# A recurrence followed by a three-matrix MLP on one core: the last 64 rows of the first product as pairs of matmuls in two row halves, and the second product in the inverse's banks

## The chip, the core and the metric

One NeuronCore of a Trainium2 chip runs the whole program. Its engines work side by side and meet at semaphores: TensorE (PE) multiplies, VectorE (DVE), ScalarE (ACT) and GpSimd (POOL) do elementwise work, SyncE (SP) issues most transfers. The metric is the device time of one execution in microseconds.

## The reference

```
for t in range(S):                       # S = 768, batch 4, 8 heads, head size 40
    y[:, :, t] = einsum('bhd,bhde->bhe', rt, state)
    Sa = einsum('bhde,bhe->bhd', state, at)
    state = state * wt[:, :, None, :] - einsum('bhd,bhe->bhde', Sa, bt) \
            + einsum('bhd,bhe->bhde', vt, kt)
x = y.transpose(0, 2, 1, 3).reshape(3072, 320)
out = ((x @ w1) * (x @ w2)) @ w3 @ w_out           # 320 -> 1024 -> 1024 -> 320
```

The recurrence's inputs are single precision; the MLP weights arrive as 64-bit numbers.

## The kernel before, in words

Time is cut into 12 chunks of 64 steps. For each chunk the recurrence is put as matrix products: `load` and `scale` bring in the inputs and form running products of the decay, `causal` forms the products of a and b (L551), `solve` inverts the small triangular matrices with a chain of VectorE instructions (L604 to L690), `join` extends these inverses to 64 steps with 32x32 matmuls (L753), `pairs` and `tokens` (L792, L816) prepare operands, and `rec` (L840) carries the state over, two of the four batches at a time. `gather` moves the result y by DMA into xr.

`mlp` then takes the chunk's 256 tokens. The 320 input columns lie as two tiles of 128 rows and one of 64 rows, which is laid out twice, in rows 0 to 63 and 64 to 127. Each factor is split in a high part (rounded for fast matmuls) and a low part. **The first product** (L957) sums, for each of 16 blocks of 128 outputs, eight matmuls of 128 rows and 256 columns over `terms`; the last two, (4, 2) and (4, 5), belong to the 64 rows: `WT[4]` holds their high part in rows 0 to 63 and their low part in rows 64 to 127, tile 2 of xs is x's high part and tile 5 its low part. **The second product** (L983) multiplies the elementwise product by W3, the product of w3 and w_out that is formed once (L470): 48 matmuls in two groups of 24, each group in one bank of PSUM, copied out as `o`.

Before the first product of the first chunk the weights must be there. `weights` converts the 64-bit numbers in pieces of 128 rows and 1024 columns (`convert`: two ScalarE and five elementwise instructions, L394 to L415, the last on DVE or POOL), 17 pieces in all, and splits w1 and w2 into high and low parts (L457). Six pieces are those of w1 and w2.

PSUM has 8 banks: six in the pool `bank`, which nearly all products share, and two that are the tile `ab` of the inverse.

The order of the work on each engine is not that of the code. Every operation is recorded with a due time and a cost, and `Order.place` sets the order of all engines once, in a list, from the tables `OFF`, `P`, `ON`, `OPS` and from the pools' sizes. On the chip each engine then runs its own list in order and waits at semaphores.

Of the kernel before, what the change touches and what calls it, by code (L numbers as in the profile page):

```python
# [14 lines left out]
ALU = mybir.AluOpType  # L15
# [4 lines left out]
NCH = S // C  # L20
# [12 lines left out]
SLOTS = dict(fm=4, xx=3, aa=3, lm=4, gi=1, gt=1, ab=1, TDX=1, rv=4, vg=5, un=4, bk=5, hs=2, st=2, y=1, xr=1, JP=2, TT=2, bank=6,  # L33
# [4 lines left out]
T0, T = 449.562, 122.639  # L38
P = dict(w0=116.83, ws=51.334, ld=75.808, sc=8.354, ca=161.389, so=-139.305, sp=243.519, jo=671.741, pa=42.027,
         tk=3.502, rg=-37.491, ga=1051.868, ml=179.371, mt=282.608)  # L40

ON = dict(aa="dppddpdddppdpppddppppddd", cv="pdddppdddpddddppp",
          gl="dpppdpppddppddpppdddddpppppdpdpdppppddddpppdpppp", ws="pdddpp", xs="ddpddppppdpppdddppddpdpd")
OFF = {"ca.j": -611.218, "ca.js": -295.116, "ca.lm": -409.432, "ca.mask": 322.878, "ca.mm": -196.496, "cv.e":
       -352.619, "cv.exp": -294.308, "cv.f": 875.871, "cv.in": 923.729, "cv.lo": 148.411, "cv.m": -331.453, "cv.out":
       -690.808, "cv.sign": -986.054, "ga": 652.698, "jo.cp1": 176.7, "jo.cp2": 1171.31, "jo.mm1": 500.308, "jo.mm2":
       559.977, "jo.tt": 1216.266, "ld.aa": 255.685, "ld.fm": -308.122, "ld.xx": -220.769, "m.a": -43.748, "m.ab":
       -25.534, "m.gh": -539.967, "m.gl": -14.3, "m.mm1": 97.143, "m.mm2": 289.0, "m.o": 98.802, "m.out": -533.298,
       "m.xh": -105.084, "m.xl": 349.579, "nil": 390.528, "pa.cp": -142.457, "pa.mask": 411.539, "pa.mm": 399.693,
       "pa.rv": 721.462, "pa.v": -32.743, "r.hs": -489.727, "r.n": 318.043, "r.s": -178.475, "r.sb": -189.193, "r.st":  # L50
       490.608, "r.t0": -269.903, "r.t1": 72.728, "r.t2": -860.309, "r.tr": -475.318, "r.u": -459.283, "r.y":
       -480.807, "r.zn": -15.068, "r.zv": -155.411, "sc.aa": 621.487, "sc.chk": -167.343, "sc.exp": 187.27, "sc.gi":
       -148.615, "sc.gt": -230.551, "sc.ln": 87.006, "sc.scan": 203.673, "sc.xs": 130.059, "so.d": -775.834, "so.in":
       -264.37, "so.m1": -358.78, "so.m2": -299.304, "so.q": 713.223, "so.sa": -515.229, "so.sb": -535.393, "so.t":
       -345.96, "so.td": 366.095, "so.tt": -385.449, "so.v": -186.183, "so.x": -90.021, "so.z": 257.847, "tk.cp":
       -717.729, "tk.mm": 348.057, "w.hi": 667.696, "w.lo": -164.398, "w3.hi": 386.505, "w3.lo": -443.484, "w3.mm":
       -484.2, "z.bk": 434.685}
LOOK = dict(pe=0.135, act=0.0, dve=0.0, pool=0.101, sp=0.0, nil=0.0)
# [1117 lines left out]
```

## Time and profile before

| | |
|---|---|
| median of 3 runs | 648.69 us (648.24 to 648.99) |
| profiled execution | 643.84 us, its span 642.1 us |
| TensorE busy | 566.2 us, 88% of the span |
| VectorE busy | 473.3 us, 74% |
| ScalarE busy | 382.5 us, 60% |
| GpSimd busy | 184.7 us, 29% |
| TensorE's granted clock, mean | 0.984 of full speed |

The span runs from the first to the last instruction; the profiled execution's own time has 1.74 us around it. Busy shares are means over stages that differ: the first quarter of the span holds the conversion of the weights, the rest the chunks' steady turn.

### The profile page before, as it was taken

To read this page: it belongs to the slowest core of one execution; us is meant where nothing else is said; L and a number is where in the kernel's file an instruction comes from. 1 tells how busy PE (TensorE), PEld (TensorE's weight loads), DVE (VectorE), ACT (ScalarE), POOL (GpSimd) and SP (SyncE) were. 2 spreads that over 40 slices of the span, in tenths; PEclk is the share of its full clock that TensorE was granted. 3 is DMA by queue.
4 is the path that set the end of the run, shared out by engine and by line. 5 is a ranking of instruction groups with operands and counts; after the bars stand their busy time and mean duration, and the time that the engine had idled before them with its cause. 6 is when DMAs were issued, how large, how long until landed. Compare 5 with 4: busy or idle time off the path is not lost.

```text
span 642.1 us, 27039 instructions
## 1 busy us (share of the span) xinstructions
PE 566.2 (88%) x11970; PEld 503.9 (78%) x11970; DVE 473.3 (74%) x849; ACT 382.5 (60%) x825; POOL 184.7 (29%) x230
## 2 busy tenths in 40 slices
PE   1536889867999999999999999998999999999995
PEld 0435767556988988888888889887988898898995
DVE  6799897987949959769589599497595794971220
ACT  6767557686465665755755746657557557354221
POOL 3542414035332413403312115332232242020111
PEclk9999989968999999999999999999999999999998
DMA  8975566535213423523534335235135333210001
GB/s 193 294 225 167 154 212 217 196 87 152 69 29 85 117 69 98 141 48 90 137 80 110 82 79 134 59 96 141 41 93 141 78 83 81 51 37 14 26 21 25
DMA packets 53401, 68.23 MB, mean 106 GB/s; under 512 B 29984, under 2 KB 37664, under 8 KB 51232
## 3 DMA queue, kind: packets, MB, share of 16 engines
q1 hardware_dynamic: 53280, 66.46, 38.3%
q8 instruction: 95, 1.56, 1.0%
q14 instruction: 26, 0.21, 0.1%
HBM read 57.79 MB, written 3.93 MB: 96 GB/s over the span
## 4 chain that ended last, share of the span: by engine, by line
PE 36%; DVE 28%; ACT 17%; DMA 9%; SPq 5%; issue 4%; POOL 0%; ACTq 0%; DVEq 0%
PE bank L957 15%; PE bank L840 9%; ACT JP L273 5%; DVE tmp L630 4%; SPq L915 4%; DMA fm<-in_fmg_dram 4%; PE bank L983 4%; ACT TT L273 3%; PE bank L551 3%; DMA xr<-y 3%; DVE ab L604 2%; PE bank L470 2%; DVE mf L408 2%; DVE ga L971 2%; ACT hs L273 2%
## 5 line engine op out<-in xcount | busy, mean ns | idle before, releaser
L957 PE MATMUL bank<-xs,W 128*128 128x256 f32 x1536 | 208.3, 288 | 2.8 <-ACT o L273 2.8
L957 PEld LDWEIGHTS bank<-xs,W 128*128 128x128 f32 x1536 | 187.8, 189 | 14.1 <-ACT o L273 3.6
L273 ACT ACTIVATE gh<-ga 128x512 fp32r<-128x512 f32 x48 | 30.3, 631 | 94.8 <-DVE ga L971 94.8
L891 DVE TENSOR_TENSOR un<-bank,mask_h 128x416 f32<-128x416 f32 x48 | 28.2, 588 | 73.0 <-PE bank L840 63.9
L974 POOL TENSOR_TENSOR gl<-ga,gh 128x512 fp32r<-128x512 f32 x29 | 37.5, 1292 | 118.3 <-ACT gh L273 92.4
L801 POOL TENSOR_SCALAR_AFFINE_SELECT vg<-vg 64x256 f32<-64x256 f32 x96 | 43.9, 457 | 74.6 <-DVE gl L974 24.0
L983 PE MATMUL bank<-W3h,gh 128*128 128x320 f32 x192 | 63.8, 332 | 0.0
L567 POOL TENSOR_SCALAR_AFFINE_SELECT lm<-lm 64x512 f32<-64x512 f32 x48 | 34.0, 708 | 95.5 <-ACT lm L273 74.7
L983 PE MATMUL bank<-W3l,gh 128*128 128x320 f32 x192 | 59.2, 308 | 0.0
L983 PE MATMUL bank<-W3h,gl 128*128 128x320 f32 x192 | 59.2, 308 | 0.0
L273 ACT ACTIVATE JP<-bank 64x256 f32<-64x256 f32 (+2 forms) x120 | 45.4, 379 | 20.7 <-PE bank L551 19.0
L840 PE MATMUL bank<-hs,TT 64*64 64x104 f32 x768 | 49.8, 269 | 7.3 <-ACT TT L273 5.2
L840 PE MATMUL bank<-un,bk 64*64 64x104 f32 (+1 forms) x768 | 47.9, 266 | 2.8 <-DVE un L891 2.3
L523 POOL TENSOR_TENSOR xx<-xx,gi 112x1024 f32<-112x1024 f32 x12 | 28.5, 2379 | 74.6 <-DVE gi L519 22.9
L971 DVE TENSOR_TENSOR ga<-bank,ga 128x512 f32<-128x512 f32 x48 | 32.7, 681 | 22.3 <-PE bank L957 22.3
L840 PEld LDWEIGHTS bank<-hs,TT 64*64 64x64 f32 x768 | 39.3, 142 | 11.5 <-ACT TT L273 6.0
L840 PE MATMUL bank<-vg,bk 64*64 64x104 f32 (+1 forms) x768 | 47.1, 264 | 0.0
L840 PEld LDWEIGHTS bank<-un,bk 64*64 64x64 f32 (+1 forms) x768 | 37.8, 130 | 8.9 <-DVE un L891 5.6
L551 PE MATMUL bank<-aa,xx 40*64 40x64 f32 x1536 | 32.8, 239 | 10.7 <-POOL xx L523 5.5
L551 PEld LDWEIGHTS bank<-aa,xx 40*64 40x64 f32 x1536 | 30.5, 153 | 12.9 <-POOL xx L523 5.7
L470 PE MATMUL bank<-wof,w3f 128*128 128x320 f32 x128 | 38.0, 453 | 2.4 <-DVE w3f L415 1.5
L273 ACT ACTIVATE ga<-bank 128x512 f32<-128x512 f32 x48 | 28.7, 597 | 16.9 <-PE bank L957 16.3
(120 smaller groups left out, 1245.9 us busy)
## 6 DMA issues: line engine op xcount, KB each, us to landing
rv<-in_rv_dram SPq DMA_DIRECT2D x48, 294.0 KB
xx<-in_fmx_dram SPq DMA_DIRECT2D x24, 448.0 KB
raw<-in_w3t_dram SPq DMA_DIRECT2D x8, 1024.0 KB
raw<-in_w_dram SPq DMA_DIRECT2D x6, 1024.0 KB
fm<-in_fmg_dram SPq DMA_DIRECT2D x24, 227.5 KB
aa<-in_fma_dram SPq DMA_DIRECT2D x24, 224.0 KB
vg<-in_vt_dram SPq DMA_DIRECT2D x48, 80.0 KB
out_dram<-o SPq DMA_DIRECT2D x48, 80.0 KB
```

The lines of the kernel that those rows point to most:

```text
L273: act.activation(out_, in_, AF.Copy, scale=scale)
L470: pe.matmul(out=pt.t[:, 0:DM], lhsT=w[:, j], rhs=wof[:, j], start=(j == 0), stop=(j == NJ - 1))
L523: e.tensor_tensor(out=X, in0=X, in1=gi.t.unsqueeze(2).to_broadcast([ROWS, 2 * NP, 2, C]), op=ALU.mult)
L551: pe.matmul(out=bank(s)[64 * z:64 * z + 64, i, p], lhsT=X[r, p, z], rhs=aa[i].t[r, p], start=True, stop=True)
L567: op("ca.mask", due + 6, lambda q=q: pool.affine_select(out=lm.t[q], in_=lm.t[q], pattern=[[0, 2 * NP], [1, C]], compare_op=ALU.is_gt, fil ...
L801: op("pa.mask", due + 2, lambda q=q, vg=vg: pool.affine_select(out=vg.t[q, :, 0:C], in_=vg.t[q, :, 0:C], pattern=[[0, NP], [1, C]], compar ...
L840: pe.matmul(out=out_(ab ^ z, p), lhsT=left(ab, ab ^ x, p), rhs=right(ab ^ x, p), start=start and p == 0, stop=True, skip_group_check=True)
L891: dve.tensor_tensor(out=un[i].t, in0=view(hp[i]), in1=mask_h.unsqueeze(1).to_broadcast([128, NP, N]), op=ALU.mult)
L957: pe.matmul(out=pt.t[:, TOK * x:TOK * x + TOK], lhsT=WT[k][:, cs], rhs=xs.t[:, z], start=(n == 0), stop=(n == 7))
L971: op("m.ab", t, lambda a=a, pt=pt: dve.tensor_tensor(out=a.t, in0=wide(pt), in1=a.t, op=ALU.mult), r=[pt], w=[a])
L974: both(("gl", c % NCH * 4 + j // 2), "m.gl", t + 1, lambda e, a=a, j=j: e.tensor_tensor(out=gl.t[:, j:j + 2], in0=a.t, in1=gh.t[:, j:j + 2 ...
L983: pe.matmul(out=pt.t[:, 0:DM], lhsT=l.t[:, j, ts], rhs=W3[r][:, j], start=(j == 0 and n == 0), stop=(j == NJ - 1 and n == 2))
```

## The change

The eighth term goes: the low part of x for the 64 rows now meets the high part of the weights alone. That product has only 64 rows, so it runs as matmuls of 64 rows: the block of w1 in row half 0 to 63 and that of w2 in row half 64 to 127, two banks at a time (`m.mm0`, four matmuls for two blocks of each, then seven terms of 128 rows for each block on top). For this `WT[4]` holds w1's high part in rows 0 to 63 and its low part below, and w2 the other way round. These 64 rows of w1 and w2 come as one piece `wc` of 128 rows instead of two pieces, so there are 16 pieces.

The second product takes its banks from a new pool `xb`, the two halves of `ab`. The solve of chunks 2 and later holds both halves, that of chunks 0 and 1 one. In the last chunk half of the output transfers are issued by ScalarE. The tables of the order are all new.

```diff
-SLOTS = dict(fm=4, xx=3, aa=3, lm=4, gi=1, gt=1, ab=1, TDX=1, rv=4, vg=5, ...
+SLOTS = dict(fm=4, xx=3, aa=3, lm=4, gi=1, gt=1, xb=2, TDX=1, rv=4, vg=5, ...
...
-T0, T = 449.562, 122.639
+T0, T = 588.06, 126.787
...
-    "m.xh": ("act", 0.9), "m.xl": ("dve", 0.95, 1), "m.mm1": ("pe", 0.95, 0, "128", 1.12, 16, 0.348, 1.88), ...
+    "m.xh": ("act", 0.9), "m.xl": ("dve", 0.95, 1), "m.mm0": ("pe", 0.25, 0, "64r", 0.43, 8, 0.08, 1.88), "m.mm1": ("pe", 0.832, 0, "128", 1.0, 14, 0.305, 1.88), ...
...
     tiles["ab"] = [ps.tile([128, 1024], F32, name="ab")]
+    tiles["xb"] = [tiles["ab"][0][:, 512 * i:512 * i + 512] for i in range(2)]
...
-            for f in range(2 * DFF // CW):
+            for f in range(2 * DFF // CW if k < 2 else 1):
                 cs = slice(CW * f, CW * f + CW)
-                mf = convert(w12[k * 128:k * 128 + 128, cs], None, due)
+                mf = convert(w12[k * 128:k * 128 + 128, cs] if k < 2 else wc, None, due)
...
+                    op("w.hi", due, f1, r=[mf, *over], w=[("W", k, x)])
+                    if k < 2:
+                        both(("ws", 2 * k + f), "w.lo", due, f2, r=[mf, *over], w=[("W", k, x)])
+                    else:
+                        op("w.lo/d", due, lambda f2=f2: f2(dve), r=[mf, *over], w=[("W", k, x)])
...
-        jp, ab, tdx = jp_[c], slot("ab"), slot("TDX")
+        jp, tdx = jp_[c], slot("TDX")
+        xbs = [slot("xb") for _ in range(1 if c < MERGED else 2)]
+        ab = xbs[0] if c < MERGED else Whole(tiles["ab"][0])
...
-    terms = [(0, 0), (0, 3), (2, 0), (1, 1), (1, 4), (3, 1), (4, 2), (4, 5)]
+    terms = [(0, 0), (0, 3), (2, 0), (1, 1), (1, 4), (3, 1), (4, 2)]
...
+            pts = [slot("bank") for _ in range(2)]
+
+            def f0(j=j, pts=pts):
+                for x in range(2):
+                    for w in range(2):
+                        q, col = slice(64 * w, 64 * w + 64), w * DFF + (j + x) * 128
+                        pe.matmul(out=pts[w].t[:, TOK * x:TOK * x + TOK], lhsT=WT[4][q, col:col + 128], rhs=xs.t[q, 5],
+                                  start=x == 0, stop=True, skip_group_check=True)
+
+            op("m.mm0", t, f0, r=[(xs, "l"), "W12"], w=pts, hold=[a, gh, gl])
...
-            pt, o = slot("bank"), slot("o")
+            pt, o = slot("xb"), slot("o")
```

What this does to the order is shown at three places. The first is TensorE's list in the steady turn. Before, a turn of the first product stands behind `join` (L753) like this, two blocks of one bank:

```order
L753 MATMUL bank_156<-TDX_119,JP_145 32x32 x32
L957 MATMUL bank_154<-xs_1832,W_0_100 128x256 x2
L957 MATMUL bank_154<-xs_1832,W_2_101 128x256
L957 MATMUL bank_154<-xs_1832,W_1_1466 128x256 x2
L957 MATMUL bank_154<-xs_1832,W_3_1467 128x256
L957 MATMUL bank_154<-xs_1832,W_4_1468 128x256 x2
L957 MATMUL bank_154<-xs_1832,W_0_100 128x256 x2
```

After, L973 is the new matmul of 64 rows, L983 what was L957, L856 what was L840:

```order
L983 MATMUL bank_155<-xs_1624,W_1_1433 128x256 x2
L983 MATMUL bank_155<-xs_1624,W_3_1434 128x256
L983 MATMUL bank_155<-xs_1624,W_4_1435 128x256
L973 MATMUL bank_153<-xs_1624,W_4_1435 128x256
L973 MATMUL bank_156<-xs_1624,W_4_1435 128x256
L973 MATMUL bank_153<-xs_1624,W_4_1435 128x256
L973 MATMUL bank_156<-xs_1624,W_4_1435 128x256
L856 MATMUL bank_158<-un_132,bk_137 64x104
L856 MATMUL bank_158<-un_132,bk_137 40x104
```

Each block has one matmul less on `W_4`, and a group of four on alternating banks stands ahead of its two banks, apart from them. Counted over the whole list up to the end of the program's normal path, the first product's matmuls of 128 rows go from 1536 to 1344, 192 of 64 rows come, and from the first of them on the stretches of one array shape (128 rows, 64 rows by 128 columns, 64 by 64, 32 by 32) number 310 where they were 262.

The second place is VectorE's list where the weights become ready. Before, the last piece's L412 is followed by the inverse of chunk 2 and by the recurrence, while POOL converts and splits the last piece:

```order
L604 STREAM_TRANSPOSE ab<-JP_144 128x1024
L412 TENSOR_TENSOR sg_165<-sg_165,e_164 128x1024
L630 TENSOR_TENSOR tmp<-GP,ab 128x4
...
L896 TENSOR_TENSOR st_140<-bank_155,fm_105 104x160
L896 TENSOR_TENSOR st_141<-bank_156,fm_105 104x160
L657 TENSOR_TENSOR tmp<-GP 128x128
L943 TENSOR_TENSOR xs_1832<-xr_143,xs_1832 128x768
```

After, L421 is that L412, L424 the last step of the conversion, L468 the split of the weights, L959 the low part of the first chunk's x:

```order
L468 TENSOR_TENSOR W_3_1434<-mf_166,W_1_1433 128x1024
L417 SCALAR_TENSOR_TENSOR mf_167<-raw_163,mf_167 128x1024
L421 TENSOR_TENSOR sg_165<-sg_165,e_164 128x1024
L424 TENSOR_TENSOR mf_167<-mf_167,sg_165 128x1024
L907 TENSOR_TENSOR un_129<-bank_158,mask_h 128x416
L468 TENSOR_TENSOR W_4_1435<-mf_167,W_4_1435 64x1024 x2
L907 TENSOR_TENSOR un_130<-bank_155,mask_h 128x416
L959 TENSOR_TENSOR xs_1624<-xr_143,xs_1624 128x768
L916 TENSOR_TENSOR y_142<-bank_157,fm_106 104x4x64
L916 TENSOR_TENSOR y_142<-bank_153,fm_106 104x4x64
L620 STREAM_TRANSPOSE ab<-JP_144 128x1024
```

The last split moved from POOL to VectorE, and chunk 2's inverse (L604, now L620) and a share of the recurrence moved behind it. Ahead of the last piece's L412 VectorE now has one piece less (four instructions, one each of L394, L404, L408, L412), two of L415, two of L891, two of L900, two of L896, one of L523 and the L604 less, and one of L457 more. TensorE's list ahead of the first product is shorter by 160 rows of L840 and 16 of L792 (each row two matmuls in the trace) and by four of L816.

The third place is VectorE's list at the turn from one inverse to the next. After, L650 is the last sum of the inverse, L706 and L709 turn it, L620 begins the next inverse in `ab`:

```order
L646 TENSOR_TENSOR tmp<-ab,GP 128x512
L650 TENSOR_REDUCE Tp<-tmp 128x8x8
L706 STREAM_TRANSPOSE TDX_119<-Tp 128x32x16
L709 STREAM_TRANSPOSE TDX_119<-TDX_119 128x512
L526 TENSOR_TENSOR aa_110<-aa_110,fm_105 112x512
L997 TENSOR_TENSOR ga_1626<-bank_153,ga_1626 128x512
L959 TENSOR_TENSOR xs_1624<-xr_143,xs_1624 128x768
L1000 TENSOR_TENSOR gl_1623<-ga_1626,gh_1622 128x512
L620 STREAM_TRANSPOSE ab<-JP_145 128x1024
L907 TENSOR_TENSOR un_129<-bank_158,mask_h 128x416
```

The rows alone stand much as they did before, but between the first and the ninth of them TensorE's 48 matmuls of the second product and ScalarE's two copies of `o` must now come and go in the same banks; before, the second product had banks of the shared pool.

## Rows read from the trace of the kernel before

**Rows 1.** The page: TensorE's busy tenths in 40 equal slices.

```profile
PE   1536889867999999999999999998999999999995
```

**Rows 2.** Windows of all engines: length, then busy us (instructions) of each, TensorE's clock, DMA.

```profile
0.00:160.00 160.00, 104.04 (x2393) 82.42 (x2394) 136.14 (x211) 109.46 (x202) 58.20 (x73) 0.95 0.66 190
160.00:590.00 430.00, 416.68 (x9128) 377.53 (x9128) 328.33 (x623) 259.91 (x601) 117.41 (x151) 1.00 0.33 85
```

**Rows 3.** The timeline where the weights become ready: start, duration, engine, line, operation.

```profile
144.90 0.68 DVE L412 TENSOR_TENSOR sg<-sg,e 128x1024 bf16<-128x1024 bf16 x1
145.73 2.13 POOL L415 TENSOR_TENSOR mf<-mf,sg 128x1024 f32<-128x1024 f32 x1 [0.74 <-DVE tmp L630]
150.49 2.35 POOL L457 TENSOR_TENSOR W<-mf,W 64x1024 fp32r<-64x1024 f32 x1 [0.18 <-ACT W L273]
156.13 0.95 DVE L943 TENSOR_TENSOR xs<-xr,xs 128x768 fp32r<-128x768 f32 x1
157.86 1.21 PE L957 MATMUL bank<-xs,W 128*128 128x256 f32 x8
```

**Rows 4.** Groups by line and shape: busy us, mean ns of one, idle before.

```profile
L394 DVE TENSOR_SCALAR e<-raw 128x1024 uint16<-128x1024 uint16 x16 | 11.2, 699 | 1.1 <-DMA raw<-in_w_dram 1.0
L408 DVE SCALAR_TENSOR_TENSOR mf<-raw,mf 128x1024 f32<-128x1024 uint32 x16 | 21.2, 1326 | 0.2
L412 DVE TENSOR_TENSOR sg<-sg,e 128x1024 bf16<-128x1024 bf16 x16 | 12.2, 760 | 3.0 <-ACT sg L401 2.4 <-ACT e L398 0.6
L415 DVE TENSOR_TENSOR w3f<-mf,sg 128x1024 f32<-128x1024 f32 x6 | 7.3, 1222 | 0.2
L891 DVE TENSOR_TENSOR un<-bank,mask_h 128x416 f32<-128x416 f32 x48 | 28.2, 588 | 73.0 <-PE bank L840 63.9 <-ACT lm L273 9.2
L900 DVE TENSOR_TENSOR y<-bank,fm 104x256 f32<-104x256 f32 x48 | 17.8, 410 | 6.1 <-PE bank L840 5.9
L896 DVE TENSOR_TENSOR st<-bank,fm 104x160 f32<-104x160 f32 x44 | 13.1, 311 | 0.0
L523 DVE TENSOR_TENSOR xx<-xx,gi 112x1024 f32<-112x1024 f32 x12 | 14.4, 1202 | 0.1
L604 DVE STREAM_TRANSPOSE ab<-JP 128x1024 f32<-128x1024 f32 x10 | 20.2, 2022 | 13.1 <-ACT JP L273 13.1
L273 ACT ACTIVATE W<-mf 128x1024 fp32r<-128x1024 f32 x6 | 6.3, 1050 | 0.6 <-DVE mf L415 0.6
```

**Rows 5.** The chain that ended last, in order of time: start, duration, what.

```profile
290.09 1.14 PE bank L957 x8
...
417.75 1.59 PE bank L840 x64
...
613.07 15.24 PE bank L957 x128
628.32 7.06 PE bank L983 x48
```

**Rows 6.** TensorE's timeline in two stretches of `rec`, which alternate between the row halves.

```profile
143.83 0.94 PE L840 MATMUL bank<-vg,lm 64*64 64x104 f32 x32 [0.17 <-ACT bk L273]
...
383.80 0.26 PE L840 MATMUL bank<-un,bk 64*40 64x104 f32 x2
383.81 0.26 PE L840 MATMUL bank<-vg,bk 64*40 64x104 f32 x2
383.89 0.26 PE L840 MATMUL bank<-un,bk 64*40 64x104 f32 x2
```

**Rows 7.** VectorE alone in one steady turn: inverse begun to turned, then up to the next.

```profile
368.30:397.50 29.20, 28.41 (x60) 1.00 0.38 99
397.50:412.50 15.00, 6.52 (x7) 1.00 0.36 89
```

**Rows 8.** The timeline's end: the last copy and the last two output transfers.

```profile
635.40 0.44 ACT L273 ACTIVATE o<-bank 128x320 f32<-128x320 f32 x1 [2.21 <-PE bank L983]
635.86 1.11 SPq L992 DMA_DIRECT2D out_dram<-o  x2
```

More of the change, by code (lines that the diff above doesn't have):

```diff
@@ L238, in place @@
             elif e == "sp":
-                done, clock[e] = max(t + FLIGHT, landed[-1]) + o["span"], t + o["cost"]
+                done, clock[e] = max(t + FLIGHT + o["cold"], landed[-1]) + o["span"], t + o["cost"]
                 landed.append(done)
+                done += o["act"]
             else:
@@ L261, in attention_moe @@
 @with_exitstack
-def attention_moe(ctx: ExitStack, tc: tile.TileContext, fmg, fmx, fma, rv, vt, sq, svr, w12, w3t, wo, out):
+def attention_moe(ctx: ExitStack, tc: tile.TileContext, fmg, fmx, fma, rv, vt, sq, svr, w12, wc, w3t, wo, out):
     nc = tc.nc
@@ L425, in convert @@
         return mf
-    pieces = iter(range(17))
+    pieces = iter(range(16))
     def weights():
@@ L445, in weights, with f1, f2 @@
                 op("nil", due, second, w=["reg2"])
-            for f in range(2 * DFF // CW):
+            for f in range(2 * DFF // CW if k < 2 else 1):
                 cs = slice(CW * f, CW * f + CW)
-                mf = convert(w12[k * 128:k * 128 + 128, cs], None, due)
-                n = (0, 1, 4)[k]
-                rows = slice(64, 128) if k == 2 else slice(0, 128)
+                mf = convert(w12[k * 128:k * 128 + 128, cs] if k < 2 else wc, None, due)
                 over = ["conv"] if k == 0 else ["conv", "reg2"]
-                def f1(mf=mf, n=n, cs=cs):
-                    copy(WT[n][:, cs], mf.t)
-                def f2(e, mf=mf, n=n, rows=rows, k=k, cs=cs):
-                    e.tensor_tensor(out=WT[2 + k][rows, cs], in0=mf.t[rows], in1=WT[n][rows, cs], op=ALU.subtract)
-                op("w.hi", due, f1, r=[mf, *over], w=[("W", k, f)])
-                both(("ws", 2 * k + f), "w.lo", due, f2, r=[mf, *over], w=[("W", k, f)])
+                for x in (f,) if k < 2 else range(2):
+                    xs = slice(CW * x, CW * x + CW)
+                    q, z = (slice(0, 128),) * 2 if k < 2 else (slice(64 * x, 64 * x + 64), slice(64 - 64 * x, 128 - 64 * x))
+                    hi, lo = (0, 1, 4)[k], 2 + k
+                    def f1(mf=mf, hi=hi, q=q, xs=xs):
+                        copy(WT[hi][q, xs], mf.t[q])
+                    def f2(e, mf=mf, hi=hi, lo=lo, q=q, z=z, xs=xs):
+                        e.tensor_tensor(out=WT[lo][z, xs], in0=mf.t[q], in1=WT[hi][q, xs], op=ALU.subtract)
+                    op("w.hi", due, f1, r=[mf, *over], w=[("W", k, x)])
[3 more added lines that the diff above has]
+                        op("w.lo/d", due, lambda f2=f2: f2(dve), r=[mf, *over], w=[("W", k, x)])
                 due += step
@@ L707, in solve @@
         for cost, fn, two in steps:
-            op("so.x", t, fn, r=[ab], w=["solve"], cost=cost, two=two)
+            op("so.x", t, fn, r=xbs, w=["solve"], cost=cost, two=two)
             t += cost * span / total
@@ L957, in f3 @@
                         pe.matmul(out=pt.t[:, TOK * x:TOK * x + TOK], lhsT=WT[k][:, cs], rhs=xs.t[:, z],
-                                  start=(n == 0), stop=(n == 7))
+                                  start=False, stop=(n == 6), skip_group_check=True)
                 for x in range(2):
@@ L991, in mlp @@
             for b in range(2):
-                op("m.out", t, lambda b=b, tt=tt, o=o: sp.dma_start(
+                tag, e = ("m.oa", act) if c == NCH - 1 and b else ("m.out", sp)
+                op(tag, t, lambda b=b, tt=tt, o=o, e=e: e.dma_start(
                     out=out[bass.ds((2 * tt + b) * S + row, C)], in_=o.t[64 * b:64 * b + 64]), r=[o])
@@ L1148, in _layout @@
     rows += [6 * D + e for e in range(8, D)] + [7 * D + e for e in range(8, D)]
-    rows += rows[256:]
     def bits(x):
```

85 lines of the change are left out of this document (45 added, 40 removed).

## The prediction

> **What bounds the kernel now.** I read the busy slices first, then windows of all engines, then the timeline where the picture changes, then the chain that ended last. The slices show a weak first quarter and a full rest [rows 1]. The windows give its size: TensorE is busy 104.0 of the first 160 us, then 416.7 of the next 430 at full clock [rows 2]. So after the first quarter TensorE bounds the kernel, with 13.3 us of gaps; before it something else does. VectorE is busy 136.1 of those 160 us, ScalarE 109.5, GpSimd 58.2 [rows 2]: the conversion of the weights, nearly all on VectorE, holds back the first product, which starts at 157.86 [rows 3]. Two things thus shorten the kernel: an earlier first product, as far as TensorE's work isn't merely moved behind it, and less TensorE time after it.
>
> In the chain, 128 matmuls of the first product take 15.24 us, 0.119 each, and 48 of the second 7.06, 0.147 each; eight of the first between stretches of another array shape take 1.14, where 8 x 0.119 is 0.95 [rows 5]. The 0.19 left over is what a change of shape costs. The recurrence starts four matmuls (each shown row stands for two) every 0.09 us [rows 6], so 64 cost 1.41 of the 1.59 that they take [rows 5], and 0.18 is left over there too. I take 0.18 a change.
>
> **The change part by part.** I cost it against the profiled execution, 643.84 us (span 642.1 and 1.74 around it); the median of the runs, 648.69, lies 4.85 above, and I carry the difference over to it unchanged.
>
> *Pairs in place of the eighth term.* Of each pair of blocks of w1 and w2, four matmuls of 128 rows go: 4 x 0.119 = 0.476 us, 48 times. Four of 64 rows come. The trace has none of that shape. Its nearest rows are the recurrence's: four matmuls of 104 columns every 0.09 us [rows 6]. One column at a time at 2.4 GHz, the higher of the clock's two levels, which the window grants [rows 2], four in turn would need 4 x 43 = 173 ns; so two must run together, and the products alternate between the row halves. Lower bound therefore: a pair costs what one does, 0.238 for the group, and 48 x 0.238 = 11.4 us are saved. Upper bound: the halves run in turn, 0.476, and nothing is saved. I take the lower, since [rows 6] are of the same kind (two row halves, alternating banks).
>
> Each of these matmuls also loads its own weights. Where all weights are 64 columns wide, 32 matmuls with their 32 loads take 0.94 us [rows 6], 0.76 without the change of shape: 2.7 columns loaded per ns. Two loads of 128 columns in 0.119 us are 2.2 per ns, so by the row the loads don't bind. The Trainium skill ("TensorE: Matmul & The Clock Gate", section LDWEIGHTS) says that a load's time goes with its columns, not its rows, columns / 1.2 in ns. By that rule two loads one after the other would take 213 ns, a group 0.43 us, and only 2 us would be saved. The trace disagrees with it for loads of two row halves, which it shows overlapping.
>
> *Changes of shape.* From the first product on, TensorE's list has 310 stretches for 262: 48 x 0.18 = 8.6 us are given back. Below, if passing from 64x64 to 64x128 is free for those groups that follow the recurrence, some 6 less; above, nothing in the trace asks for more than 0.19.
>
> *The start.* Ahead of the last piece's L412 VectorE has less to do: a piece without its last step (L394 and L404 at 0.70 each, L408 1.33, L412 0.76), two L415 (2.44), two L891 (1.18), two L900 (0.82), two L896 (0.62), an L523 (1.20), an L604 (2.02), less one L457, priced as the like-shaped L415 (1.22) [rows 4]: 11.8 - 1.2 = 10.6 us. VectorE is 85% busy there [rows 2], so I let its idle time stand and count 10.6. Behind L412, before: 11.2 us to L943, mostly two slow steps on GpSimd and another before them (2.13, 2.35) [rows 3]. After: L412 0.76, L415 1.22, ScalarE's first half 1.05, two L457 on VectorE 2.44 [rows 4], then what lies between the last split and L943, 3.3 before (150.49 + 2.35 to 156.13, [rows 3]) and at least one ScalarE copy, say 1; I take 2. Together 7.5, so 3.7 earlier (2.5 to 4.7). The first product starts 14.3 us earlier.
>
> *What the start leaves behind.* TensorE's list ahead of the first product is shorter by 176 rows of L840 and L792, 352 matmuls at 0.022: 7.7 us come after it instead. (L816's four are about made up for by the shorter 40-column ones.)
>
> *The inverse's banks.* The second product (7.06 us a chunk, [rows 5]) and the copies of `o` must fit between the last read of `ab` and the next L604, and everything in VectorE's list behind L604, the masks L891 of the recurrence first, waits with it. In a steady turn L604 to L690 takes 29.2 us, 28.4 of it busy, and 15.0 pass to the next L604, 6.5 busy [rows 7]. The new stay is 7.1 for the matmuls, 0.4 for the copy [rows 8], 3.2 for `join` (128 matmuls at 0.022 and two changes), 0.9 for a block of the recurrence between, 0.5 for changes: 12.1 of 15.0. VectorE's idle time there covers it, with 3 us to spare; cost 0, and what it takes if the cover is gone is a rival below. The banks it frees in the shared pool gain nothing by the trace's steady gaps, 13.3 us in all.
>
> *The end.* The last two transfers are issued by one queue in 1.11 us [rows 8]; two issuers save half, 0.5.
>
> Sum: -14.3 + 7.7 - 11.4 + 8.6 - 0.5 = -9.9. Profile 643.84 to 633.9; median 648.7 to **638.8 us**. Bounds of the single terms make it 632 (free changes, the start 1 us better) to 650 (pairs in turn).
>
> **The rivals.**
> - *The pairs don't overlap.* Then the 11.4 is gone: 650. For it: no such shape is in the trace. Against it: [rows 6]. Chance 0.08. The Trainium skill's rule on loads above, with both halves loaded in turn, would come out close to this, at 648.
> - *The start gains little.* If ScalarE (109 of 160 us busy) or the transfers of the raw pieces set the pace once VectorE has less between them, the first product comes 6 us earlier, not 14.3: -1.6, 647. For it: L412 already waits 3.0 us for ScalarE [rows 4]. Against: that is little in 16 pieces. Chance 0.15.
> - *Slower: the inverse and the second product wait for each other.* Place: L604 behind the copy of `o`. If TensorE gets through the 12.1 us late because its blocks wait in their turn for VectorE (L891 waits 63.9 us for TensorE over the run, [rows 4]), each microsecond beyond the 15.0 lengthens every turn, some ten of them. From 1 us a turn it eats the whole gain; at 2 us it is -9.9 + 20 = +10, 659. For it: VectorE is 97% busy in L604 to L690, so it can't catch up. Against: 3 us of room. Chance 0.16.
> - *The forecast*, 0.61, with its own range of 630 to 645.
>
> **How the numbers follow.** 638.8 is the likeliest case's time. The range 628 to 654 takes in the free changes and a better start below, the pairs in turn, the small start and half of the slower rival above. A change of 0.2% (1.3 us) is about what a measurement of this kernel can tell. Faster: the forecast (0.61), the small start (0.12 of its 0.15), part of the rest 0.03: 0.76. Same: 0.03 and 0.04 of the pairs, 0.07. Slower: 0.16 and a small rest, 0.17.
>
> **What would show it.** In the profile after: the first product starting near 143.5 instead of 157.9; groups of L973 of four matmuls that take about 0.42 with their change of shape, not 0.66; about 0.18 more for each block of the first product that they precede; a steady turn near 44 us or a little less; VectorE's wait at L620 behind ScalarE's `o` of some microseconds that costs TensorE nothing; the masks L907 not waited for longer than before. The prediction is wrong if the first product starts after 152, if L973's group takes over 0.6, or if the turn is above 45 with TensorE idle ahead of L856 while VectorE stands at L620.

## The result, and the profile after

| | before | after |
|---|---|---|
| median of the runs | 648.47 us (647.37 to 648.99) | 639.44 us (638.80 to 640.05) |
| ratio, 95% interval | | 0.9863 (0.9846 to 0.9880) |
| span of the profiled execution | 642.1 us | 638.0 us |

The change gains 9.0 us, 1.4%; 9.9 were forecast. The profiled execution of before lay 4.6 us under the median of its runs, that of after did not; so the kernel of before was run and profiled again (`before_again`, 648.2 us, span 645.7), and stretches are compared with this second profile where nothing else is said. How far one profile can mislead shows in the two of before: they differ by 1.6 us up to chunk 3's inverse and by 1.9 over the eight turns behind it.

The page of the kernel after, with the slices that answer to [rows 1] and two groups that answer to [rows 4]:

```profile
span 638.0 us, 27026 instructions
...
PE   1535988869999999999999999999999999999996
...
L907 DVE TENSOR_TENSOR un<-bank,mask_h 128x416 f32<-128x416 f32 x48 | 28.1, 585 | 30.6 <-PE bank L856 30.5
...
L620 DVE STREAM_TRANSPOSE ab<-JP 128x1024 f32<-128x1024 f32 x10 | 20.1, 2009 | 28.5 <-ACT o L281 24.6
```

VectorE's wait for the recurrence's products (L907, before L891) fell from 63.9 to 30.5 us; a new one came, 24.6 us of the inverse's first instruction behind ScalarE's copy of `o`.

The timeline after. It answers to [rows 3] (first seven lines), shows one turn from an inverse's end to the next inverse's begin (263.35 to 275.03), the new matmuls of 64 rows (592.90 on), and answers to [rows 8] (last lines):

```profile
135.62 0.69 DVE L421 TENSOR_TENSOR sg<-sg,e 128x1024 bf16<-128x1024 bf16 x1
138.69 2.47 DVE L468 TENSOR_TENSOR W<-mf,W 64x1024 fp32r<-64x1024 f32 x2 [0.51 <-ACT W L281]
142.54 0.96 DVE L959 TENSOR_TENSOR xs<-xr,xs 128x768 fp32r<-128x768 f32 x1 [0.75 <-ACT xs L956]
144.25 1.95 DVE L620 STREAM_TRANSPOSE ab<-JP 128x1024 f32<-128x1024 f32 x1
145.04 0.49 PE L973 MATMUL bank<-xs,W 64*128 64x256 f32 x1
145.68 0.50 PE L973 MATMUL bank<-xs,W 64*128 64x256 f32 x3 [0.16 <-ACT bk L281]
189.16 2.05 DVE L620 STREAM_TRANSPOSE ab<-JP 128x1024 f32<-128x1024 f32 x1 [1.81 <-ACT JP L281]
...
263.35 1.15 DVE L706 STREAM_TRANSPOSE TDX<-Tp 128x512 f32<-128x512 f32 x1
264.53 2.55 ACT L281 ACTIVATE TT<-TDX 32x512 f32<-32x512 f32 x4
274.56 0.44 ACT L281 ACTIVATE o<-ab 128x320 f32<-128x320 f32 x1
275.03 1.99 DVE L620 STREAM_TRANSPOSE ab<-JP 128x1024 f32<-128x1024 f32 x1 [8.34 <-ACT o L281]
...
592.90 0.50 PE L973 MATMUL bank<-xs,W 64*128 64x256 f32 x4
593.33 3.55 PE L983 MATMUL bank<-xs,W 128*128 128x256 f32 x28
...
609.39 0.74 PE L973 MATMUL bank<-xs,W 64*128 64x256 f32 x8
610.06 2.14 PE L983 MATMUL bank<-xs,W 128*128 128x256 f32 x16
...
632.62 0.44 ACT L281 ACTIVATE o<-ab 128x320 f32<-128x320 f32 x1 [1.24 <-PE ab L1009]
633.09 0.48 ACTq L1019 DMA_DIRECT2D out_dram<-o  x1
```

The last piece's L421 (L412 before) comes at 135.62 for 144.90, the first product at 145.04 for 157.86. Four matmuls of 64 rows start at 592.90 and the next stretch at 593.33: 0.43 with their change of shape. Eight in a row take 0.67 (609.39 to 610.06), so four cost 0.24 and one change of shape 0.19. The group at 592.90 lies between two stretches of 128 rows and so brings two changes: by the starts of the matmuls around it, it puts those behind it off by 0.61, about 0.24 and twice 0.19.

The same moments in the second profile of before: chunk 2's inverse at 144.87 with the last piece of the weights (L412) still inside it, the first product at 159.10, chunk 3's inverse at 195.73:

```profile
144.87 1.99 DVE L604 STREAM_TRANSPOSE ab<-JP 128x1024 f32<-128x1024 f32 x1
146.77 0.77 DVE L412 TENSOR_TENSOR sg<-sg,e 128x1024 bf16<-128x1024 bf16 x1
159.10 1.21 PE L957 MATMUL bank<-xs,W 128*128 128x256 f32 x8
...
195.73 2.00 DVE L604 STREAM_TRANSPOSE ab<-JP 128x1024 f32<-128x1024 f32 x1 [0.78 <-ACT JP L273]
```

Windows cut at the inverses: chunk 2's inverse, then up to chunk 3's, then the eight turns from chunk 3's to chunk 11's. Columns as in [rows 2]. Before (second profile):

```profile
144.87:178.84 33.97, 30.26 (x534) 27.91 (x534) 29.92 (x59) 19.75 (x44) 15.62 (x15) 0.95 0.40 110
178.84:195.73 16.89, 15.39 (x421) 14.13 (x419) 6.36 (x9) 11.63 (x25) 5.80 (x6) 1.00 0.15 32
195.73:548.97 353.24, 342.82 (x7675) 308.93 (x7675) 273.74 (x523) 220.25 (x512) 102.17 (x132) 1.00 0.36 94
```

After, with the two windows that answer to [rows 2] ahead and the two halves of one turn behind (inverse, then up to the next), as in [rows 7]:

```profile
0.00:160.00 160.00, 103.99 (x2240) 82.70 (x2244) 135.94 (x208) 108.73 (x197) 56.42 (x70) 0.94 0.61 178
160.00:590.00 430.00, 416.82 (x9419) 372.61 (x9413) 328.27 (x624) 267.84 (x605) 117.29 (x153) 1.00 0.34 87
144.25:174.54 30.29, 29.02 (x590) 25.65 (x589) 27.08 (x55) 17.14 (x40) 9.63 (x14) 0.98 0.42 115
174.54:189.16 14.62, 14.29 (x376) 12.98 (x376) 5.97 (x8) 11.55 (x26) 6.11 (x5) 1.00 0.21 52
189.16:542.16 353.00, 340.62 (x7713) 304.35 (x7715) 278.08 (x532) 226.45 (x514) 100.61 (x132) 1.00 0.36 94
320.86:350.69 29.83, 28.63 (x622) 25.80 (x614) 28.30 (x59) 17.55 (x41) 10.80 (x14) 1.00 0.49 132
350.69:363.36 12.67, 11.90 (x267) 10.17 (x269) 4.67 (x7) 10.97 (x23) 2.49 (x3) 1.00 0.08 17
```

The gain is nearly all in one turn, that of chunk 2. Chunk 2's inverse begins 0.6 us earlier, its turn takes 44.9 us for 50.9 (30.29 + 14.62 for 33.97 + 16.89), and so chunk 3's inverse comes 6.6 earlier. The eight turns behind it give 0.2 (353.00 for 353.24), the stretch from chunk 11's inverse to the last copy takes 0.7 more (542.16 to 632.62 for 548.97 to 638.70), and the end from that copy on gives 1.6 (638.0 - 632.62 for 645.7 - 638.70). Together 7.7 of span, as 645.7 to 638.0 says. Against the first profile of before, that turn gains as much (44.9 for 51.1), and the eight turns behind it lose 1.7. What went is what the turn of chunk 2 had over a steady one: 6.7 us before (50.9 for 44.15), 0.8 after. TensorE is about as busy in the eight turns as before, 96% and 97%.

### The profile page after: what moved, and what is told of

Same layout as the page of the kernel before. It is cut to its first block, busy times and chain, and to the rows that moved or that the text cites. A ratio compares the mean times of both kernels' runs of the same rounds, so it can differ in the third digit from the quotient of the medians.

```text
span 638.0 us, 27026 instructions
## 1 busy us (share of the span) xinstructions
PE 562.5 (88%) x11970; PEld 494.6 (78%) x11970; DVE 474.9 (74%) x849; ACT 388.4 (61%) x823; POOL 177.6 (28%) x225
## 4 chain that ended last, share of the span: by engine, by line
DVE 34%; PE 30%; ACT 15%; DMA 5%; issue 5%; SPq 2%; POOL 0%; ACTq 0%; DVEq 0%; POOLq 0%
PE bank L983 10%; PE ab L1009 7%; DVE tmp L646 7%; PE bank L856 6%; ACT JP L281 4%; ACT TT L281 3%; DMA fm<-in_fmg_dram 3%; DVE ab L620 3%; DVE ab L650 2%; DVE ga L997 2%; DVE fm L516 2%; PE bank L565 2%; DVE un L907 2%; DVE y L916 2%; DVE Tp L650 2%
## 5 line engine op out<-in xcount | busy, mean ns | idle before, releaser
L983 PE MATMUL bank<-xs,W 128*128 128x256 f32 x1344 | 189.9, 289 | 0.0
L983 PEld LDWEIGHTS bank<-xs,W 128*128 128x128 f32 x1344 | 166.1, 188 | 10.1 <-issue 0.6
L817 POOL TENSOR_SCALAR_AFFINE_SELECT vg<-vg 64x256 f32<-64x256 f32 x96 | 45.2, 471 | 103.9 <-ACT vg L281 52.3
L1000 POOL TENSOR_TENSOR gl<-ga,gh 128x512 fp32r<-128x512 f32 x25 | 32.1, 1286 | 146.6 <-ACT gh L281 95.2
L1009 PE MATMUL ab<-W3h,gh 128*128 128x320 f32 x192 | 62.8, 327 | 3.2 <-ACT o L281 3.2
L1009 PE MATMUL ab<-W3h,gl 128*128 128x320 f32 x192 | 59.4, 309 | 0.2 <-DVE gl L1000 0.2
L1009 PE MATMUL ab<-W3l,gh 128*128 128x320 f32 x192 | 59.2, 308 | 0.0
L856 PE MATMUL bank<-hs,TT 64*64 64x104 f32 x768 | 50.4, 266 | 7.5 <-ACT TT L281 6.3
L907 DVE TENSOR_TENSOR un<-bank,mask_h 128x416 f32<-128x416 f32 x48 | 28.1, 585 | 30.6 <-PE bank L856 30.5
L856 PE MATMUL bank<-un,bk 64*64 64x104 f32 (+1 forms) x768 | 47.1, 262 | 2.2 <-DVE un L907 2.1
L856 PEld LDWEIGHTS bank<-hs,TT 64*64 64x64 f32 x768 | 39.2, 140 | 12.6 <-ACT TT L281 8.7
L856 PE MATMUL bank<-vg,bk 64*64 64x104 f32 (+1 forms) x768 | 46.8, 262 | 0.1
L856 PEld LDWEIGHTS bank<-un,bk 64*64 64x64 f32 (+1 forms) x768 | 37.2, 128 | 9.0 <-DVE un L907 3.9
L537 POOL TENSOR_TENSOR xx<-xx,gi 112x1024 f32<-112x1024 f32 x13 | 31.0, 2384 | 47.0 <-DVE gi L533 24.2
L620 DVE STREAM_TRANSPOSE ab<-JP 128x1024 f32<-128x1024 f32 x10 | 20.1, 2009 | 28.5 <-ACT o L281 24.6
```

The lines of the kernel that those rows point to most:

```text
L620: dve.transpose(out=ab.t.rearrange("q (t r p) -> q t r p", r=2, p=16), in_=src)
L817: op("pa.mask", due + 2, lambda q=q, vg=vg: pool.affine_select(out=vg.t[q, :, 0:C], in_=vg.t[q, :, 0:C], pattern=[[0, NP], [1, C]], compar ...
L856: pe.matmul(out=out_(ab ^ z, p), lhsT=left(ab, ab ^ x, p), rhs=right(ab ^ x, p), start=start and p == 0, stop=True, skip_group_check=True)
L907: dve.tensor_tensor(out=un[i].t, in0=view(hp[i]), in1=mask_h.unsqueeze(1).to_broadcast([128, NP, N]), op=ALU.mult)
L983: pe.matmul(out=pt.t[:, TOK * x:TOK * x + TOK], lhsT=WT[k][:, cs], rhs=xs.t[:, z], start=False, stop=(n == 6), skip_group_check=True)
L1009: pe.matmul(out=pt.t[:, 0:DM], lhsT=l.t[:, j, ts], rhs=W3[r][:, j], start=(j == 0 and n == 0), stop=(j == NJ - 1 and n == 2))
```

## The experiments

In the first eight kernels VectorE, ScalarE and GpSimd run their instructions in the order of the kernel that they start from, doubled instructions aside (by the traces one VectorE instruction moved in `before_7terms` and one in `before_inverse_plus`), so one thing changes at a time. "Turn" is an eighth of the time from chunk 3's inverse to chunk 11's, "rest" the time from chunk 11's inverse to the span's end, all from the profiled execution; the difference is that of the medians, from 639.44 for kernels made from after, from 647.33, before's median beside them, for the two made from before. Beside the kernels made from after, before had medians of 648.87 (the three of the pairs) and 647.33, and 648.47 beside after itself, so a microsecond of their differences isn't read.

| kernel | median, us | difference | chunk 3's inverse | turn | rest |
|---|---|---|---|---|---|
| before, first profile | 648.47 | | 194.10 | 43.92 | 96.7 |
| `before_again` | 648.20 | | 195.73 | 44.15 | 96.7 |
| `before_7terms` | 645.13 | -2.2 | 193.96 | 44.24 | 95.1 |
| `before_inverse_plus` | 653.80 | +6.5 | 198.37 | 44.67 | 97.4 |
| after | 639.44 | | 189.16 | 44.13 | 95.8 |
| `no_pairs` | 632.95 | -6.5 | 188.99 | 43.89 | 91.3 |
| `full_rows` | 639.14 | -0.3 | 190.02 | 44.05 | 95.5 |
| `pairs_in_turn` | 643.03 | +3.6 | 187.76 | 44.39 | 97.5 |
| `inverse_plus` | 651.37 | +11.9 | 189.70 | 45.21 | 96.9 |
| `copies_plus` | 653.70 | +14.3 | 191.38 | 45.53 | 96.5 |

**The kernel of before once more.**

> The kernel before, unchanged, profiled once more. Its profiled execution on record lies 4.6 us under the median of its runs, that of the changed kernel does not lie under its own. Theory: the two kernels are 9 us apart in every execution, and the first profile of before was a lucky one; this profile then shows 646 to 649 us, and the difference to the first profile sits in one place: more TensorE time at the lower clock level or longer gaps ahead of the first product (over 160 us for it where it was 157.9). Rival: the difference is spread over the steady turns (44.3 us each in the first profile, then 44.7).

The ratio to before is 0.9998 (0.9964 to 1.0031). Single executions of this kernel spread from 645.77 to 653.17, so differences under 2 us between medians aren't read here. Neither expectation holds as it stands: of the 3.6 us between the two profiles half lies ahead of chunk 3's inverse (the first product comes at 159.10, not after 160) and half in the steady turns (44.15 for 43.92).

**What the pairs of 64 rows are worth.** Three edits of `f0` and `f3` in `mlp`. Without the four matmuls (their part of the product is left out):

```diff
             def f0(j=j, pts=pts):
-                for x in range(2):
...
+                return
...
-                                  start=False, stop=(n == 6), skip_group_check=True)
+                                  start=(x == 0 and n == 0), stop=(n == 6), skip_group_check=True)
```

> The changed kernel with the groups of four 64-row matmuls left out; the product of x's low part with the last 64 rows of the weights is thus not computed. All else stands in the same order on every engine. TensorE's list has 192 matmuls and 57 stretches of one shape less. Theory (TensorE bounds the run behind the first product; a group costs 0.24 us, a change of shape 0.18): 11.4 + 10.3 = 21.7 us less than the changed kernel, 618 us. Rival (the turn between the inverse and the second product, or VectorE's list, bounds it): less than half of that, 629 us or more, with TensorE's gaps grown by what its work shrank.

Measured 632.95, ratio to before 0.9760 (0.9700 to 0.9819). The time that TensorE spends on the groups in after is 48 x 0.43 = 20.6 us; 6.5 came off, 4.5 of them in the rest and 1.9 in the eight turns (351.14 for 353.00). The window of these turns:

```profile
188.99:540.13 351.14, 330.61 (x7610) 296.46 (x7605) 277.63 (x532) 225.68 (x514) 100.42 (x132) 1.00 0.37 95
```

TensorE is 10.0 us less busy there and the turns are 1.9 shorter, as much as two profiles of one kernel differ: the rest became gaps, as the rival has it. In one of these turns (405.72 to 449.62) the granted clock's mean fell to 0.96, and that turn is 1.7 longer than in after; the other seven are 3.5 shorter together. So well under half of TensorE's time came off here.

With the eighth term back as a matmul of 128 rows, and no groups (`WT[4]`'s rows are those of after, so this term isn't the one of before):

```diff
-    terms = [(0, 0), (0, 3), (2, 0), (1, 1), (1, 4), (3, 1), (4, 2)]
+    terms = [(0, 0), (0, 3), (2, 0), (1, 1), (1, 4), (3, 1), (4, 2), (4, 5)]
...
+                return
...
-                                  start=False, stop=(n == 6), skip_group_check=True)
+                                  start=(x == 0 and n == 0), stop=(n == 7), skip_group_check=True)
```

> The changed kernel with the eighth term back as a matmul of 128 rows at the end of each block and no groups of 64 rows; the weights' layout, the inverse's banks and the order stay. Theory: 192 matmuls of 0.119 more (22.8), the groups' 11.4 and 57 changes of shape (10.3) less: +1 us, 640.5, so that the pairs by themselves bring next to nothing. Rival (a change of shape costs much less than 0.18 next to a group of 64 rows): +5 us or more, 645.

Measured 639.14, ratio 0.9864 (0.9806 to 0.9922): the same as after, as the theory has it. The pairs, which are what the change is about, bring nothing here.

With both matmuls of a pair in row half 0 to 63 (the second then reads the other half's data):

```diff
-                        q, col = slice(64 * w, 64 * w + 64), w * DFF + (j + x) * 128
+                        q, col = slice(0, 64), w * DFF + (j + x) * 128
```

> The changed kernel with both matmuls of a pair in row half 0 to 63, so that they can't run side by side; for w2 the 64 rows then hold the weights' low part, so that term is another one. Order, counts and banks are the same. Theory (two row halves overlap, 0.238 for a group; in turn 0.476): +11.4 us, 651. Rival (the halves already run in turn, by the loads of their weights): no change, 639.5.

The timeline, the same place as the 592.90 above:

```profile
594.25 0.73 PE L973 MATMUL bank<-xs,W 64*128 64x256 f32 x4
594.91 3.55 PE L983 MATMUL bank<-xs,W 128*128 128x256 f32 x28
```

A group takes 0.66 for 0.43; less the 0.19 of the change of shape, four matmuls cost 0.47 in one half and 0.24 in two. The halves do overlap. Of the 48 x 0.23 = 11.0 us that TensorE lost, the kernel lost 3.6: 643.03, ratio 0.9932 (0.9899 to 0.9965).

**What holds the turn.** If TensorE's time doesn't come off, something else holds the 44 us. The first kernel is that of before without the eighth term, whose part of the product is left out:

```diff
-    terms = [(0, 0), (0, 3), (2, 0), (1, 1), (1, 4), (3, 1), (4, 2), (4, 5)]
+    terms = [(0, 0), (0, 3), (2, 0), (1, 1), (1, 4), (3, 1), (4, 2)]
...
-                                  start=(n == 0), stop=(n == 7))
+                                  start=(n == 0), stop=(n == 6))
```

> The kernel of before without the eighth term of the first product (L957): 192 matmuls of 0.119 us go, 22.8 us of TensorE time, so part of the product is left out of the output. Theory A (TensorE bounds the kernel after the first quarter, as the prediction said): -22.8, to about 626 us, and the turn from one inverse to the next falls from 44.15 to about 42. Theory B (the steady turn is held by the inverse on VectorE and the copies on ScalarE behind it, as the run without the pairs suggests for the changed kernel): the turn stays within 0.3 us of 44.15, and only the last part, behind the last inverse, gets shorter: -5 to -9, 640 to 643 us.

Measured 645.13, ratio 0.9952 (0.9910 to 0.9994). The eight turns:

```profile
193.96:547.86 353.90, 331.75 (x7553) 295.28 (x7552) 274.44 (x522) 219.69 (x512) 102.02 (x132) 1.00 0.36 94
```

TensorE is 11.1 us less busy than in the second profile of before (331.75 for 342.82) and the turns take 0.7 more. Inside the eight inverses (L604 to L690) it has 222.4 us to do for 231.6, and they take 235.0 for 234.7. Theory A is out, for the kernel of before already; B's size for the rest was too large too, 1.6 us. The rest in two parts, up to the first product behind the last inverse's copies and from there to the end of TensorE's work, in the second profile of before and here:

```profile
548.97:584.70 35.73, 34.21 (x708) 30.79 (x707) 28.15 (x58) 17.25 (x41) 3.30 (x8) 1.00 0.16 40
584.70:638.67 53.97, 53.97 (x642) 51.61 (x642) 11.36 (x20) 14.56 (x27) 9.06 (x7) 1.00 0.09 21
...
547.86:586.24 38.38, 34.85 (x695) 30.79 (x693) 28.12 (x58) 17.36 (x41) 3.30 (x8) 0.96 0.15 37
586.24:636.20 49.96, 49.96 (x610) 47.61 (x610) 11.36 (x20) 14.55 (x27) 9.03 (x7) 1.00 0.09 23
```

In the second part, where TensorE has no gap, 32 matmuls less take 4.0 us less, all of their time (32 x 0.119 = 3.8). In the first part 2.7 us are lost, and there the granted clock's mean is 0.96 for 1.00.

Next, one instruction more in each of the ten inverses, the widest product, in after and in before:

```diff
-                dve.tensor_tensor(out=scratch(*shape), in0=x().to_broadcast([128, *shape]),
-                                  in1=y().to_broadcast([128, *shape]), op=ALU.mult)
+                for _ in range(2 if n == 1024 else 1):
+                    dve.tensor_tensor(out=scratch(*shape), in0=x().to_broadcast([128, *shape]),
+                                      in1=y().to_broadcast([128, *shape]), op=ALU.mult)
```

> The changed kernel with the inverse's product of 1024 columns on VectorE issued twice, to the same effect: one more instruction of 1.22 us in each of the ten inverses, TensorE's work as it was. Theory A (TensorE bounds): VectorE's idle time in a turn, some 8 us, takes it, 0 to +2 us, 639 to 641. Theory B (the turn is held by the inverse): each turn gets 1.22 us longer, +11 to +13, 650 to 652 us.

> The same doubled instruction of the inverse in the kernel of before: +1.22 us of VectorE time in each of ten inverses. If the inverse holds the turn before the change too: +11 to +13 us. If TensorE bounded the kernel before and the inverse's ring took its place only with the change: 0 to +4 us.

In after 651.37, +11.9 (ratio to before 1.0071, 1.0037 to 1.0106): the turn grows by 1.08 of the 1.22 us put in. (In one of the eight turns, 323.89 to 368.45, the granted clock's mean is 0.96 and the turn 2.1 longer; the other seven grow by 0.95 each.) In before 653.80, +6.5 (1.0094, 1.0065 to 1.0122): 0.5 a turn, between the two expectations. The inverse is on the path in both, in after for most of what was put in, in before for less than half. Where the other half went shows when the turn is cut in two: in after the inverse (up to L706) gets 1.17 longer and the stretch behind it stays (15.3 for 15.4); in before the inverse (up to L690) gets 1.15 longer and the stretch behind it 0.64 shorter (14.2 for 14.8). So in before that stretch holds waits that take up part of a delay.

Last, more work for ScalarE behind the inverse, two of the four copies TT<-TDX twice:

```diff
+            def fill(r=r, q=q):
+                for _ in range(2 if q > 1 else 1):
+                    copy(tt.t[r, :, 32 * (q % 2):32 * (q % 2) + 32], half(0)[r])
```

> The changed kernel with two of the four copies TT<-TDX on ScalarE, behind each inverse, issued twice to the same effect: some 1.25 us of ScalarE time more in each turn. If the ring that holds the turn goes inverse, ScalarE's copies, next inverse: +10 to +13 us, 649 to 652. If ScalarE's copies run beside other waits (TensorE's, the solve of the next chunk's inputs): 0 to +3 us.

Measured 653.70, +14.3 (ratio to before 1.0103, 1.0068 to 1.0138), the turn +1.40. That is more than was put in: in two turns (369.12 to 416.96 and 460.50 to 509.93) the granted clock's mean is 0.96 and 0.97, and they are 2.4 and 2.7 longer; the other six grow by 1.0 each. ScalarE's timeline in the turn that is shown above for after:

```profile
267.71 3.88 ACT L281 ACTIVATE TT<-TDX 32x512 f32<-32x512 f32 x6
271.60 1.54 ACT L281 ACTIVATE JP<-bank 32x256 f32<-32x256 f32 x4
273.16 0.44 ACT L281 ACTIVATE o<-ab 128x320 f32<-128x320 f32 x1
274.38 0.60 ACT L281 ACTIVATE lm<-bank 128x512 f32<-128x512 f32 x1 [0.79 <-PE bank L565]
275.00 1.16 ACT L281 ACTIVATE JP<-bank 64x256 f32<-64x256 f32 x3
276.20 1.27 ACT L281 ACTIVATE JP<-JP 32x512 f32<-32x512 f32 x2
277.48 1.55 ACT L281 ACTIVATE TT<-bank 32x256 f32<-32x256 f32 x4
279.05 0.44 ACT L281 ACTIVATE o<-ab 128x320 f32<-128x320 f32 x1
```

From the first copy to the end of `o` ScalarE has one gap of 0.79 us. After took 264.53 to 275.00 for this, 10.5 us; here it is 267.71 to 279.49, 11.8, and the next L620 follows at 279.52. That is the ring: the inverse on VectorE (28.30 of 29.83 us busy in the window above), then a row of small copies on ScalarE (10.97 of 12.67), then the next inverse. The turns of after are not all alike: the stretch behind the inverse takes from 11.7 to 18.6 us, the longer ones with more ScalarE instructions (32 to 37 for 23). Over all eight, VectorE is busy 220.1 of 229.7 us in the inverses and ScalarE 107.9 of 123.3 behind them. In seven of the eight the next L620 starts 0.03 us behind the end of an `o`, in the eighth, at 497.79, as close behind the copies JP<-JP. (In some of these turns VectorE works on masks, L907, until then, so that hardly any wait is shown; the 24.6 us are nearly all in three turns.) TensorE has a part in the ring too: some of these copies wait for its products, 0.79 us in the turn shown.

**The parts of the start, apart.** Four kernels were to tell what the 6.6 us in the first turn are made of: `weights_alone`, before with the one piece `wc` and nothing else (first lines below); `old_tables`, after with before's numbers for the order; `start17`, after with `wc` converted twice (second lines); `banks_alone`, before with the second product in `xb` (third).

```diff
-    pieces = iter(range(17))
+    pieces = iter(range(16))
...
-    pieces = iter(range(16))
+    pieces = iter(range(17))
...
-            pt, o = slot("bank"), slot("o")
+            pt, o = slot("xb"), slot("o")
```

"The third chunk's inverse" in these expectations is chunk 3's, counted from 0.

> The kernel of before with one part of the change alone: the last 64 rows of both weights come as one piece, split in halves, so that 16 pieces are converted for 17; the order's numbers, the eighth term and the banks are as before. One piece takes VectorE about 3.5 us (L394, L404, L408, L412) and ScalarE some 3. Theory S (the start carries the gain, and what comes earlier there comes earlier at the end): the third chunk's inverse comes 3 to 5 us earlier and the kernel ends 3 to 5 us earlier, 643 to 645. Theory O (the gain is the new order of the whole list): -1 to 0, 647 to 648.5.

> The changed kernel in all its parts, with the numbers of before for the order (T0, P, ON, OFF, LOOK). Theory S (the parts carry the gain by the shorter conversion): 639 to 644. Theory O (the new order carries it): 646 to 652, with the third chunk's inverse no earlier than before.

> The changed kernel with the piece of the last rows converted twice, once for each half, so that 17 pieces are converted again; all else is as after the change. Theory S (start counts one for one): the first product and the third chunk's inverse 3 to 5 us later, and the kernel +3 to +5, 642 to 645. Theory O (the conversion has room and the new order carries the gain): 0 to +1, 639 to 641.

> The kernel of before with the second product in the inverse's two banks and nothing else changed (order numbers, eighth term and 17 pieces as before). By the prediction the move costs and gains nothing: 647 to 650. Rival 1 (it ties the next inverse to the copies of the second product, a term of the ring that holds the turn): +4 to +20, the turn over 44.6. Rival 2 (the freed banks let the first product run ahead): -2 to -5.

| kernel | median, us | ratio to before, 95% | VectorE's instructions that keep the order of the kernel it is made from |
|---|---|---|---|
| `weights_alone` | 673.23 | 1.0411 (1.0338 to 1.0484) | 651 of 847 |
| `old_tables` | 712.62 | 1.1069 (1.0994 to 1.1143) | 574 of 847 |
| `start17` | 708.15 | 1.0971 (1.0890 to 1.1051) | 639 of 854 |
| `banks_alone` | 687.33 | 1.0590 (1.0486 to 1.0693) | 639 of 849 |

All four lie far outside both theories, 26 to 65 us slower than before. What they have in common shows in the last column: each edit changes what `Order.place` weighs, and a quarter to a third of VectorE's instructions (23 to 32%, by the longest sequence that two traces share) come to stand elsewhere. So these runs don't tell the parts apart, and that the orders alone made them slow is not shown. Chunk 3's inverse comes at 192.60 in `start17`, 3.4 later than in after, as Theory S has it, and at 192.67 in `old_tables`, earlier than before, against Theory O; with the orders moved neither is read as a price. In `banks_alone` the turn is 49.8 us, and its L614 (the L604) waits 42.2 us for `o`, as its first rival has it, though past its bound and with the order moved too. One of the four still says something about the start, `weights_alone`:

```profile
144.05 1.48 PE L962 MATMUL bank<-xs,W 128*128 128x256 f32 x8 [0.41 <-ACT SB L273]
...
177.14 1.95 DVE L609 STREAM_TRANSPOSE ab<-JP 128x1024 f32<-128x1024 f32 x1 [1.51 <-ACT JP L273]
242.54 2.00 DVE L609 STREAM_TRANSPOSE ab<-JP 128x1024 f32<-128x1024 f32 x1
```

Its first product starts 15.0 us earlier than in the second profile of before, and chunk 3's inverse 18.6 earlier; chunk 4's, 65 us later, is then 4.4 late (242.54 for 238.12). An early first product, and even an early inverse of chunk 3, is worth nothing if the order loses it again right behind.

## Why the prediction was right, and which step failed

The total was right, 638.8 for 639.44, and the term that carries it was right in size: the start less what it leaves behind, -14.3 + 7.7 = -6.6, and chunk 3's inverse does come 6.6 us earlier (4.9 against the first profile, 194.10). That the two agree to the tenth is luck: the 7.7 supposes that TensorE's work is what is waited for, which the steady turns contradict. The other terms were to give -3.3; they give 1.1 of span. The signs that the prediction named came (first product at 145.04, groups at 0.43, the turn at 44.13, L620 behind `o`), but none of them could tell whether TensorE bounds the turn.

**The step that failed** is the first sentence drawn from the windows: "So after the first quarter TensorE bounds the kernel". TensorE is busy for 97% of the eight turns, and yet 11.1 us less of its work there changed their length by +0.7 us, while in the kernel after 1.22 us more in each inverse added 8.7 and some 1.25 us more of copies behind each 11.2. TensorE's list fills the ring's length; it doesn't make it. Its time counts where no inverse follows, in the rest, which ends on TensorE [rows 5]: there `no_pairs` gained 4.5 of its 6.5 us, and behind the last inverse's copies `before_7terms` got all the time of its 32 matmuls back. In after this ring is shown by both doublings; in before the inverse's doubling gave 0.5 a turn of 1.22, the copies were not doubled there, and what else holds its turn stays open. The Trainium skill ("Perfetto Trace Analysis", section Identifying the Most-Contended Engine) warns that the busy share of matmuls is no good measure of how close a kernel is to roofline and points to the share of peak arithmetic and to the busy share of the weight loads. The second would not have saved the step here: the loads are busy 308.93 of 353.24 us, more than VectorE's 273.74, and by the page's advice, to optimize the most contended engine first, TensorE would still be chosen.

- *Pairs, -11.4.* Right on TensorE: 0.24 a group, the lower bound taken. Wrong as a price of the kernel, since `full_rows`, without them, takes 639.14. The rival "the pairs don't overlap" at 650 was mis-sized by the same step: forced, it gives 643.03. Of the rule on loads that the prediction weighed, in the Trainium skill's "TensorE: Matmul & The Clock Gate" (section LDWEIGHTS), the estimate with one load after the other was 0.43 us for the four; the traces show 0.24 in two halves, against it, and 0.47 in one.
- *Changes of shape, +8.6.* Right on TensorE: 0.19 each for 0.18, two of them where a group lies between stretches of 128 rows, and no more on the path than the pairs.
- *The start, -14.3.* Measured -12.8 from the same rows: L421 9.3 us earlier for 10.6, and 3.5 for 3.7 behind it; -14.1 against the second profile.
- *What it leaves behind, +7.7.* The size holds with the start's, the reason isn't borne out: in the steady turns TensorE is not what is waited for, and in `before_7terms`, with less TensorE work, chunk 2's turn is no shorter (51.2 us for 50.9, at a granted clock of 0.86 for 0.95 in its inverse). By the windows the turn of chunk 2 gets shorter: in the inverse VectorE has 2.8 us less to do (27.08 for 29.92) and 0.8 less idle time, and the stretch behind it is 2.3 shorter. The granted clock makes little of it: in `full_rows`, whose order is that of after, its mean is 0.94 in that inverse, before 0.95, and the inverse takes 30.8 us for 34.0. How much is the shorter conversion and how much the new order of the lists stays open; the four last kernels didn't settle it.
- *The banks, 0.* Right in the sum: L620 waits for `o` 24.6 us, as foreseen, and the turn is 44.13 for 44.15. Wrong in the reason: there are no "3 us to spare". `copies_plus` shows that a longer row of copies ahead of `o` delays the next inverse in full. The rival that ends slower named the right ring; it closes at the length that the turn had already.
- *The end, -0.5.* It gives 1.3 against the first profile (6.7 to 5.4 from the last copy to the span's end), 1.6 against the second. Why more than the second issuer's half microsecond was not tried.

## What to carry to other kernels

An engine that is busy for 97% of a stretch need not be its bound where engines run fixed lists in a ring: take some of its work out, or double one instruction of another engine, before a microsecond of it is priced at a microsecond. Read a steady stretch by cutting windows at the moments that recur; here VectorE is dense in one piece and ScalarE in the next, each about half idle in the other, and these two are the ones to shorten, while TensorE, dense in both, was not the bound. And where numbers set the order for one exact set of operations, an edit of a part changes the order as well, and its time says little about the part.

## What the runs showed of the hardware

Two row halves of TensorE work at once for matmuls of 64 rows, 128 weight columns and 256 moving columns: four in 0.24 us, 0.47 in one half. Each change of shape costs 0.19, so that a group of four between two stretches of 128 rows takes 0.61.

The four orders that take longer also run at a lower clock: the granted clock's mean over the span is 0.92 to 0.96 in their profiles, 0.98 in after's. In `old_tables` the window that answers to [rows 2] reads:

```profile
160.00:590.00 430.00, 380.44 (x8211) 338.27 (x8214) 298.47 (x566) 236.45 (x545) 107.49 (x145) 0.90 0.31 82
```

The granted clock's mean is 0.90, between the two levels of 1.2 and 2.4 GHz, where after holds 1.00; TensorE is busy 380 us there for 417. Gaps and the lower clock came together; how much of this kernel's 73 us over after each of them made was not measured.
